# k and q of six attention units loaded in 2-KB packets and transposed by products with columns of the identity, two-bank score operations, early weight stores moved later, and a new opening order

## Chip, core and metric

The kernel runs on one core of one Trainium2 chip. The metric is the device time of one execution in microseconds (us).

## What is computed

```
a   = softmax over each 64-token chunk of q k^T / 8        q, k, v: 4 x 8 heads x 576 x 64, fp32
x   = a v, heads put side by side                          2304 tokens x 512
y   = ((x w_a) * (x w_b)) w_out                            512 -> 1536 -> 512
out = (P(h) / (Q(h) + 1e-6)) w_out2,  h = y w_in2          512 -> 2048 -> 512
```

P is a cubic polynomial of h, Q a quadratic one of |h|.

## The kernel before

All matmuls of the two MLPs are done in three products of a high and a low part (mm3, L251 to L253). TensorE (PE) is the engine that this keeps busy for nearly the whole program.

Tokens are handled in 18 units of 128 (two chunks of 64, all 8 heads). For a unit, `a_load` (L324) fetches k, q and v as [128 tokens, 8 heads, 64], so each packet is one head's 64 numbers of one token: 256 bytes. `a_transpose` (L333, L335) turns k and q into [head pair and d, token] with four 128x128 transposes on PE and one ACT copy out of PSUM. `a_scores` (L350) makes the scores with 16 products of 64x64 into two PSUM banks, a and b; DVE takes the maximum and subtracts it, once per bank (L356, L358). Then come the exponential (ACT, L364), sum, reciprocal and scaling (DVE, L369 to L372), the transposition of the probabilities (L380, L382) and the product with v (`a_pv`, L397), whose result is split into x_hi (ACT, L402) and x_lo (DVE, L406).

Units 0 to 2 make the first 384 tokens. The first product of the first MLP (L251, tile ab) needs all three of them and the first weight tile. Units 3 to 5 are done between products of ab, the later units in pairs (a_scores2, L430 to L438; a_pv2, L473).

A weight tile (512 KB) is loaded by SP (L170), recombined from its fp32 words and split in four pieces (`w_piece`: ACT L216, L218, L225; DVE L220, L223, L233; then L192 and L197 as hi and lo). Its recombined copy w_x is stored to DRAM by POOL (L235) right away, 256 KB each, since a later stage reads it back (L600).

The order of the opening is written out by hand in two strings. LOADS is the order of SP's first transfers (w is the next weight tile). FIRST is the order in which the pieces are issued: kN, qN are transpositions, SN scores, XN exponential, EN the rest of the softmax, PN transposition, VN product with v, LN the low part, w a weight piece, dN N dummy products (L898) on PE, +kN a load. Behind FIRST, work is queued with a due time (`later`, `todo`), and `tick` runs what is due; `half` lets 0.5 of that time pass after each half of an ab product. Each engine runs its own instructions in the order of issue.

Of the kernel before, what the change touches and what calls it, by code (L numbers as in the profile page):

```python
# [9 lines left out]
F32 = mybir.dt.float32  # L10
F32R = mybir.dt.float32r
I32 = mybir.dt.int32
# [3 lines left out]
ALU = mybir.AluOpType  # L16
# [4 lines left out]
def chunk_attention_two_mlps(  # L21
# [57 lines left out]

    FIRST = "k0 q0 w w d2 S0 w X0 w k1 E0 d2 q1 S1 w X1 P0 k2 w q2 E1 V0 w S2 X2 L0 w d2 P1 w V1 d4 +k5 E2 +v4 +q5 +v3 w w L1 P2 d2 +v5 w V2 d4 w L2 w w".split()  # L80
    LOADS = "k0 q0 w k1 q1 w v0 k2 q2 v1 w w v2 k3 q3 k4 q4".split()

    AHEAD = 4
    NWP = 12 - AHEAD
# [17 lines left out]
    ps_acc = ctx.enter_context(tc.tile_pool(name="ps_acc", bufs=4, space=PSUM))  # L102
    ps_ab = ctx.enter_context(tc.tile_pool(name="ps_ab", bufs=1, space=PSUM))
    ps_at = ctx.enter_context(tc.tile_pool(name="ps_at", bufs=2, space=PSUM))

    y_d = dram.tile([P, KD, NT], F32, name="y_d", tag="y_d")
# [87 lines left out]
    def w_lo(n):  # L194
        if n in f32s:
            hi, lo = wt[order[n]]
            nc.vector.tensor_tensor(lo, f32s.pop(n).bitcast(F32), hi.bitcast(F32), ALU.subtract)  # L197
            whole.add(order[n])

    def w_piece():  # L200

# [60 lines left out]
    def later(dt, f):  # L262
        todo.append((now[0] + dt, n_todo[0], f))
        n_todo[0] += 1
# [35 lines left out]
    def a_load(u, *names):  # L300

        (b0, c0), (b1, c1) = divmod(2 * u, NCH), divmod(2 * u + 1, NCH)
        for nm, src in (("k", k), ("q", q), ("v", v)):
# [19 lines left out]
            for dst, s in parts:  # L323
                nc.sync.dma_start(out=dst, in_=s.rearrange("h s d -> s h d"))  # L324
            raw[nm, u] = t

    def a_transpose(u, nm):

        t = raw.pop((nm, u)).rearrange("p (a b) d -> p a (b d)", b=2)
# [55 lines left out]
    def a_pv(u):  # L385

        pT, vv = un.pop(("pT", u)), raw.pop(("v", u))
        ps = []
        for c in range(2):
            pool, tag = (ps_acc, "acc") if u < UH else (ps_ab, "ab"[c])  # L390
            ps.append(pool.tile([P, HP, CH], F32, name="at", tag=tag))
        for hp in range(HP):
            a, t = divmod(hp, 2)
            for c in range(2):
                for h2 in range(2):
# [3 lines left out]
                    )  # L399
        out = [[t[:, :, u * P + c * CH:u * P + (c + 1) * CH] for t in (x_hi, x_lo)] for c in range(2)]  # L400
        for c, (hi, lo) in enumerate(out):
            nc.scalar.copy(hi, ps[c])  # L402
# [16 lines left out]
    def a_scores2(u):  # L419

        qT, kT = un["both", "qT"], un["both", "kT"]
        ps = [ps_ab.tile([P, 2, HP, CH], F32, name="at", tag=tag) for tag in "ab"]
        for x in range(2):
# [10 lines left out]
        e = a_both(u, "e").rearrange("p u x (y d) -> p u (x y) d", d=CH).rearrange("p u (b x) d -> p u b x d", b=2)  # L434
        for b in range(2):
            nc.vector.tensor_reduce(m[:, b], ps[b], AX.X, ALU.max)
        for b in range(2):
            nc.vector.tensor_tensor(  # L438
                e[:, :, b], ps[b], m[:, b].unsqueeze(3).to_broadcast([P, 2, HP, CH]), ALU.subtract
            )  # L440
# [72 lines left out]
    def x_second(g):  # L513
# [450 lines left out]
    def s_begin():  # L964

        nonlocal p_j2
        s_t.close()
        p_j2 = s_t.enter_context(tc.tile_pool(name="j2", bufs=1, side="right", reuse_waits="tile"))
        s_load(0)
        s_load(1)  # L970
# [175 lines left out]
```

## Time and profile before

| | us |
|---|---|
| median of 3 runs | 891.0 |
| lowest, highest | 889.84, 893.25 |
| the profiled execution, its own time | 891.69 |
| its span in the trace | 889.9 |
| PE busy | 872.8 (98%) |
| DVE, ACT busy | 717.8 (81%), 609.9 (69%) |

The profiled execution is the one that the trace shows; its own time is the span and 1.8 us around it, and it lies 0.7 us over the median. Shares of busy time are means over stages with different limits: the opening (to about 25 us) is a chain through all engines, and behind it PE hardly ever waits.

### The profile page before, as it was taken

What the parts mean: (1) busy time and instruction counts of PE and PEld (TensorE: products, weight loads), DVE (VectorE), ACT (ScalarE), POOL (GpSimd) and SP (SyncE); (2) the same over time, 40 slices, a digit from 0 to 9 for tenths busy, and PEclk for the clock granted to TensorE, in tenths of its full rate; (3) what the DMA queues carried; (4) which work ended last, traced back from release to release, by engine and by line L of the source; (5) the groups of instructions that cost most, each with busy time, mean ns of one, the idle gap of its engine ahead of it and who ended that gap; (6) DMA issues with size and microseconds to landing.
All of it is one profiled execution on the core that took longest, in us unless ns stands there. A gap on an engine that the chain in (4) does not pass through costs nothing.

```text
span 889.9 us, 14704 instructions
## 1 busy us (share of the span) xinstructions
PE 872.8 (98%) x5528; PEld 782.3 (88%) x5528; DVE 717.8 (81%) x1273; ACT 609.9 (69%) x1091; POOL 64.6 (7%) x122
## 2 busy tenths in 40 slices
PE   5989999999999999999999999999999999999998
PEld 4889999999999999888888998888888888888997
DVE  6757896767887885578877699999889888988886
ACT  6867987444555443577886788877677767776875
POOL 0112121111111111000100000000000000000000
PEclk9999999999999999999999999999999999999999
DMA  9999985134443335478876200200020002000100
GB/s 242 256 292 267 263 236 159 69 119 148 131 148 124 125 105 192 133 255 280 287 267 233 72 1 1 83 1 1 1 95 1 1 1 84 0 1 1 48 1 36
DMA packets 107335, 105.82 MB, mean 119 GB/s; under 512 B 61440, under 2 KB 84480, under 8 KB 107264
## 3 DMA queue, kind: packets, MB, share of 16 engines
q1 hardware_dynamic: 99264, 79.71, 30.3%
q0 software_dynamic: 8000, 25.17, 7.5%
q8 instruction: 43, 0.70, 0.3%
q14 instruction: 28, 0.23, 0.1%
HBM read 74.98 MB, written 29.88 MB: 118 GB/s over the span
## 4 chain that ended last, share of the span: by engine, by line
PE 93%; ACT 2%; DMA 2%; DVE 1%; SPq 1%; issue 0%; ACTq 0%
PE h L251 7%; PE h L253 7%; PE h L252 7%; PE acc L253 7%; PE acc L252 7%; PE acc L251 7%; PE acc L765 5%; PE acc L766 5%; PE acc L768 5%; PE ab L251 3%; PE ab L252 3%; PE ab L253 3%; PE y L252 3%; PE y L253 3%; PE y L251 3%; PE q L251 2%
## 5 line engine op out<-in xcount | busy, mean ns | idle before, releaser
L253 PE MATMUL h<-y,w_i 128*128 128x512 f32 (+1 forms) x320 | 117.7, 368 | 0.0
L251 PE MATMUL h<-y,w_i 128*128 128x512 f32 (+1 forms) x320 | 117.7, 368 | 0.0
L252 PE MATMUL h<-y,w_i 128*128 128x512 f32 (+1 forms) x320 | 117.6, 368 | 0.0
L823 ACT ACTIVATE a_ring<-h 128x512 f32<-128x512 f32 (+1 forms) x80 | 44.1, 551 | 85.9 <-PE h L253 85.9
L662 ACT COPY s<-y 128x384 f32<-128x384 f32 x72 | 34.5, 480 | 85.2 <-PE y L253 85.0
L765 PE MATMUL acc<-g_hi,w_o 128*128 128x512 f32 (+1 forms) x240 | 86.4, 367 | 0.0
L766 PE MATMUL acc<-g_hi,w_o 128*128 128x512 f32 (+1 forms) x240 | 86.2, 367 | 0.0
L826 DVE SCALAR_TENSOR_TENSOR u<-u,cb_t,a_ring 128x512 f32<-128x512 f32 (+1 forms) x80 | 55.6, 695 | 29.4 <-ACT u L824 28.8
L252 PE MATMUL acc<-w_o,g_hi 128*128 128x512 f32 x191 | 74.4, 390 | 0.0
L253 PE MATMUL acc<-w_o,g_lo 128*128 128x512 f32 x191 | 74.4, 389 | 0.0
L251 PE MATMUL acc<-w_o,g_hi 128*128 128x512 f32 x191 | 74.3, 389 | 0.0
L251 PEld LDWEIGHTS h<-y,w_i 128*128 128x128 f32 x320 | 60.1, 188 | 8.6
L252 PEld LDWEIGHTS h<-y,w_i 128*128 128x128 f32 x320 | 60.0, 188 | 8.6
L253 PEld LDWEIGHTS h<-y,w_i 128*128 128x128 f32 x320 | 60.1, 188 | 7.6
L745 DVE TENSOR_TENSOR g_lo<-g_raw,g_hi 128x512 fp32r<-128x512 f32 (+1 forms) x60 | 38.2, 638 | 30.8 <-PE acc L768 15.0
L768 PE MATMUL acc<-g_lo,w_o 128*128 128x512 f32 (+1 forms) x240 | 59.0, 367 | 0.0
L825 ACT ACTIVATE t<-h,ca_t 128x512 f32<-128x512 f32 (+1 forms) x80 | 59.0, 737 | 0.0
L836 DVE SCALAR_TENSOR_TENSOR u<-u,r 128x512 f32<-128x512 f32 (+1 forms) x80 | 50.6, 632 | 9.1 <-ACT r L835 9.1
L828 DVE SCALAR_TENSOR_TENSOR t<-t,ca_t,h 128x512 f32<-128x512 f32 (+1 forms) x80 | 55.6, 695 | 2.8
L835 ACT ACTIVATE r<-r,nlsh 128x512 f32<-128x512 f32 (+1 forms) x80 | 54.5, 682 | 2.6
L834 ACT ACTIVATE r<-u,nlsh 128x512 f32<-128x512 f32 (+1 forms) x80 | 55.5, 694 | 0.5
L837 DVE SCALAR_TENSOR_TENSOR t<-t,ca_t,r 128x512 f32<-128x512 f32 (+1 forms) x80 | 55.4, 692 | 0.0
(210 smaller groups left out, 2380.6 us busy)
## 6 DMA issues: line engine op xcount, KB each, us to landing
w_raw<-in_moe_w_out_dram SPq DMA_DIRECT2D x28, 512.0 KB, 3.9
g_d<-g POOLq DMA_DIRECT2D x72, 192.0 KB, 2.5
g_raw<-g_d SPq DMA_DIRECT2D x48, 256.0 KB, 4.0
w_raw<-in_moe_w_in_dram SPq DMA_DIRECT2D x16, 512.0 KB, 4.2
w_raw<-in_moe_w_a_dram SPq DMA_DIRECT2D x12, 512.0 KB, 5.7
w_raw<-in_moe_w_b_dram SPq DMA_DIRECT2D x12, 512.0 KB, 5.5
out_dram<-o SPq DMA_DIRECT2D x18, 256.0 KB, 2.3
y_d<-ys POOLq DMA_DIRECT2D x16, 256.0 KB, 3.5
```

The source lines that it names most:

```text
L251: nc.tensor.matmul(ps, wh, xh, start=first, stop=False, **kw)
L252: nc.tensor.matmul(ps, wh, xl, start=False, stop=False, **kw)
L253: nc.tensor.matmul(ps, wl, xh, start=False, stop=last, **kw)
L765: nc.tensor.matmul(acc[j][d], wh, gh, start=i == 0, stop=False)
L766: nc.tensor.matmul(acc[j][d], wl, gh, start=False, stop=False)
L768: nc.tensor.matmul(acc[j][d], cols(w, d)[0], gl, start=False, stop=i == F1 - 1)
L825: nc.scalar.activation(t, ps, AF.Identity, scale=ca_t[:, 3:4], bias=ca_t[:, 2:3])
L826: nc.vector.scalar_tensor_tensor(u, u, cb_t[:, 0:1], ah, ALU.add, ALU.mult)
L828: nc.vector.scalar_tensor_tensor(t, t, ca_t[:, 1:2], ps, ALU.add, ALU.mult)
L834: nc.scalar.activation(r, u, AF.Ln, scale=2.0 ** -LSH, bias=nlsh[:, 0:1])
L835: nc.scalar.activation(r, r, AF.Exp, scale=-1.0, bias=nlsh[:, 1:2])
L837: nc.vector.scalar_tensor_tensor(t, t, ca_t[:, 0:1], r, ALU.add, ALU.mult)
```

## The change

1. **2-KB rows.** With KQ = 6, units 0 to 5 load k and q with partition = (head, group of 8 tokens) and 8 tokens x 64 numbers in a row, 2 KB in one piece. The source's access pattern is then 8 heads x 16 groups x 512 numbers (8 x 8 x 512 for the halves of unit 4, which lies over two batches), where it was 128 tokens x 8 heads x 64. v and the other units load as before.
2. **Transposition by products.** Such a tile is turned by 16 plain products (8 tokens of a group x 2 halves) of the tile's 128 x 64 column block with 64 columns of the identity, in place of four transposes. Each writes 64 partitions of the bank; the two halves of a pair write the lower and the upper 64. The ACT copy reads PSUM with a step of 64 numbers to put the tokens back in order.
3. **Two-bank operations.** Scores go to one tile of two banks. One DVE maximum and one subtraction of 512 numbers replace two of 256 each; in pairs one maximum of 1024 replaces two of 512. x_hi and x_lo of units 3 to 5 become one operation each.
4. **Stores later.** The w_x of the first 8 weight tiles are held in rooms of the X pool (w_room), and their stores are queued for time 9 + n.
5. **Order.** New FIRST and LOADS; the operations of `x_second` for the groups of units before the last are paced over 14 half-steps, not 13.

```diff
-    FIRST = "k0 q0 w w d2 S0 w X0 w k1 E0 d2 q1 S1 w X1 P0 k2 w q2 E1 V0 w S2 X2 L0 w d2 P1 w V1 d4 +k5 E2 +v4 +q5 +v3 w w L1 P2 d2 +v5 w V2 d4 w L2 w w".split()
-    LOADS = "k0 q0 w k1 q1 w v0 k2 q2 v1 w w v2 k3 q3 k4 q4".split()
+    FIRST = "k0 q0 w d2 w w S0 w X0 k1 E0 d2 q1 S1 w X1 P0 w k2 q2 E1 V0 w S2 L0 d2 w X2 P1 d2 w +k5 E2 w +v4 +v3 V1 +q5 d4 w w L1 P2 d2 +v5 V2 d4 w L2 w w w".split()
+    LOADS = "k0 q0 w k1 q1 w v0 k2 v2 k3 q2 v1 w k4 q3 w q4".split()
+    KQ = 6
...
+    def w_room(n):
+
+        if n >= NWP:
+            return p_io.tile([P, DM], I32, name="w_x", tag="io")
+        if n % 3 == 0:
+            rooms[n // 3] = p_X.tile([P, 3, DM], I32, name="w_x", tag=f"X1_{(7, 6, 4)[n // 3]}")
+        return rooms[n // 3][:, n % 3]
...
-            x = f32s[n] = p_io.tile([P, DM], I32, name="w_x", tag="io")
+            x = f32s[n] = w_room(n)
             nc.vector.tensor_tensor(x, c, z, ALU.add)
             if key in w1_d:
-                nc.gpsimd.dma_start(out=w1_d[key], in_=x.bitcast(F32))
+                def store():
+                    nc.gpsimd.dma_start(out=w1_d[key], in_=x.bitcast(F32))
+
+                if n < NWP:
+                    todo.append((9 + n, n_todo[0], store))
+                    n_todo[0] += 1
+                else:
+                    store()
...
-                nc.sync.dma_start(out=dst, in_=s.rearrange("h s d -> s h d"))
+                if nm == "v" or u >= KQ:
+                    nc.sync.dma_start(out=dst, in_=s.rearrange("h s d -> s h d"))
+                elif b0 == b1:
+                    nc.sync.dma_start(
+                        out=dst.rearrange("p h d -> p (h d)"), in_=s.rearrange("h (g j) d -> h g (j d)", j=H)
...
-        for hp in range(HP):
-            nc.tensor.transpose(ps[:, hp, :], t[:, hp, :], ident)
         o = a_tmp(u, nm + "T") if u < 2 * UH else a_both(u, nm + "T")[:, u % 2]
-        nc.scalar.copy(o, ps)
+        if u >= KQ:
+            t = t.rearrange("p (a b) d -> p a (b d)", b=2)
+            for hp in range(HP):
+                nc.tensor.transpose(ps[:, hp, :], t[:, hp, :], ident)
+            nc.scalar.copy(o, ps)
+        else:
+
+            same = 2 * u // NCH == (2 * u + 1) // NCH
+            ps = ps.rearrange("p a (x y) -> p (a x) y", x=2)
+            if same:
+                eye = ident.rearrange("p (a b g) -> p b a g", a=HP, b=2)
+            else:
+                eye = ident.rearrange("p (c a b g) -> p b a c g", c=2, a=HP, b=2)
+            for j in range(H):
+                for b in range(2):
+                    r = slice(b * CH, (b + 1) * CH)
+                    nc.tensor.matmul(ps[r, j], t[:, j], eye[:, b], start=True, stop=True)
+            nc.scalar.copy(o.rearrange("p a (g j) -> p (a g) j", j=H), ps.rearrange("p j y -> p y j"))
...
+    def two_banks(n):
+
+        t = ps_two.tile([P, 2, 2 * HP, CH], F32, name="at", tag="two")
+        return t[:, :, :n * HP], [t[:, b, :n * HP] for b in range(2)]
...
-        ps = [ps_ab.tile([P, HP, CH], F32, name="at", tag=tag) for tag in "ab"]
+        two, ps = two_banks(1)
...
-        for b in range(2):
-            nc.vector.tensor_reduce(m[:, b], ps[b], AX.X, ALU.max)
-        for b in range(2):
-            nc.vector.tensor_tensor(
-                e[:, b], ps[b], m[:, b].unsqueeze(2).to_broadcast([P, HP, CH]), ALU.subtract
-            )
+        nc.vector.tensor_reduce(m, two, AX.X, ALU.max)
+        nc.vector.tensor_tensor(e, two, m.unsqueeze(3).to_broadcast([P, 2, HP, CH]), ALU.subtract)
...
-            pool, tag = (ps_acc, "acc") if u < UH else (ps_ab, "ab"[c])
-            ps.append(pool.tile([P, HP, CH], F32, name="at", tag=tag))
+        if u >= 3:
+            two, ps = two_banks(1)
+        else:
+            pool, tag = (ps_acc, "acc") if u < UH - 0 else (ps_at, "at")
+            ps = [pool.tile([P, HP, CH], F32, name="at", tag=tag) for c in range(2)]
...
-            later(at + 0.5 * (n * (9 if g == NQ - 1 else 13) // len(ops)) + (1.5 if g == NQ - 1 and n >= 7 else 0), f)
+            later(at + 0.5 * (n * (9 if g == NQ - 1 else 14) // len(ops)) + (1.5 if g == NQ - 1 and n >= 7 else 0), f)
```

SP's queue from its seventh transfer on, that is v of unit 0, before (kqv is the tile of a unit's k, q or v, w_raw that of a weight):

```order
L324 DMA kqv<-in_v_dram 128x8x64
L324 DMA kqv<-in_k_dram 128x8x64
L324 DMA kqv<-in_q_dram 128x8x64
L324 DMA kqv<-in_v_dram 128x8x64
L170 DMA w_raw<-in_moe_w_a_dram 128x4x256
L170 DMA w_raw<-in_moe_w_b_dram 128x4x256
```

and now:

```order
L345 DMA kqv<-in_v_dram 128x8x64
L347 DMA kqv<-in_k_dram 128x1x512
L345 DMA kqv<-in_v_dram 128x8x64
L347 DMA kqv<-in_k_dram 128x1x512
L347 DMA kqv<-in_q_dram 128x1x512
L345 DMA kqv<-in_v_dram 128x8x64
L173 DMA w_raw<-in_moe_w_a_dram 128x4x256
L351 DMA kqv<-in_k_dram 64x1x512 x2
```

q of unit 2, the third row before, is now the fifth: v of unit 2 and k of unit 3 go ahead of it. The weight tile that was the fifth row is now the seventh.

PE's first instructions before (at is a PSUM tile; t holds kT, qT or the probabilities of a unit, ident is the identity):

```order
L333 MATMUL at<-ident,kqv 128x128 x8
L898 MATMUL at<-ident 128x128 x2
L350 MATMUL at<-t_144 64x64 x16
L333 MATMUL at<-ident,kqv 128x128 x4
L898 MATMUL at<-ident 128x128 x2
L333 MATMUL at<-ident,kqv 128x128 x4
L350 MATMUL at<-t_145 64x64 x16
```

and now:

```order
L378 MATMUL at<-ident,kqv 64x64 x32
L947 MATMUL at<-ident 128x128 x2
L399 MATMUL at<-t_144 64x64 x16
L378 MATMUL at<-ident,kqv 64x64 x16
L947 MATMUL at<-ident 128x128 x2
L378 MATMUL at<-ident,kqv 64x64 x16
L399 MATMUL at<-t_145 64x64 x16
```

Nothing changes its place here; each transposition of four instructions became one of sixteen (the size shown is that of the result). Between the products of ab the transpositions of units 3 to 5 stand where they stood.

POOL's first stores before (w_a and w_b in DRAM are written from w_x):

```order
L235 DMA w_a_118<-w_x 128x512
L235 DMA w_b_119<-w_x 128x512
L235 DMA w_a_120<-w_x 128x512
L576 DMA g_d_83<-g 128x384
L235 DMA w_b_121<-w_x 128x512
L235 DMA w_a_122<-w_x 128x512
L576 DMA g_d_84<-g 128x384
```

and now:

```order
L625 DMA g_d_83<-g 128x384
L625 DMA g_d_84<-g 128x384
L625 DMA g_d_85<-g 128x384
L625 DMA g_d_86<-g 128x384
L249 DMA w_a_118<-w_x 128x512
L249 DMA w_a_126<-w_x 128x512
L625 DMA g_d_83<-g 128x384
L249 DMA w_b_119<-w_x 128x512
L249 DMA w_a_120<-w_x 128x512
L249 DMA w_b_127<-w_x 128x512
```

The first store of a weight tile now follows the fourth store of g, and the stores of the first eight tiles alternate with those of the later ones.

## Rows read from the trace of the kernel before

**Rows 1.** Windows by stage: us; busy of PE, PEld, DVE, ACT, POOL; clock; DMA share; GB/s

```profile
0.00:25.00 25.00, 15.55 (x261) 12.79 (x261) 15.89 (x41) 15.78 (x30) 2.38 (x9) 1.00 1.01 242
25.00:40.00 15.00, 14.96 (x177) 13.68 (x177) 10.86 (x27) 12.27 (x23) 1.70 (x4) 1.00 0.95 254
40.00:56.00 16.00, 13.07 (x162) 10.78 (x162) 10.46 (x23) 10.94 (x24) 2.70 (x5) 1.00 1.00 294
56.00:150.00 94.00, 93.27 (x1251) 88.84 (x1252) 75.71 (x125) 77.93 (x140) 16.93 (x31) 1.00 0.88 243
```

**Rows 2.** Waits of PE, 25 to 150 us: us in total, times, longest

```profile
PE at L333 <- DMA kq<-in_k_dram: 1.5, 1, 1.5
PE at L333 <- DMA q<-in_q_dram: 0.9, 1, 0.9
PE ab L251 <- ACT w_b L192: 0.4, 1, 0.4
```

**Rows 3.** Timeline of PE, opening: start, us, operation [idle before it, what ended it]

```profile
4.08 1.09 PE L333 MATMUL at<-ident,kqv 128*128 128x128 f32 x4 [4.08 <-DMA kqv<-in_k_dram]
5.60 1.12 PE L333 MATMUL at<-ident,kqv 128*128 128x128 f32 x4 [0.43 <-DMA kqv<-in_q_dram]
...
7.50 1.13 PE L350 MATMUL at<-t 64*64 64x64 f32 x32
...
13.81 1.27 PE L333 MATMUL at<-ident,kqv 128*128 128x128 f32 x8 [0.44 <-DMA kqv<-in_k_dram]
...
16.70 0.69 PE L350 MATMUL at<-t 64*64 64x64 f32 x32 [0.80 <-ACT t L335]
...
24.95 0.42 PE L251 MATMUL ab<-x_hi,w_a 128*128 128x384 f32 x1
```

**Rows 4.** Timeline of ACT, opening

```profile
6.75 0.58 ACT L335 COPY t<-at 128x512 f32<-128x512 f32 x1 [0.96 <-PE at L333]
7.55 0.79 ACT L216 ACTIVATE w_a<-w_raw 128x512 f16<-128x512 f32 x1 [0.21 <-DMA w_raw<-in_moe_w_a_dram]
```

**Rows 5.** Timeline of DVE, opening

```profile
12.61 0.76 DVE L356 TENSOR_REDUCE m<-at 128x4 f32<-128x256 f32 x2
13.28 0.75 DVE L358 TENSOR_TENSOR t<-at,m 128x256 f32<-128x256 f32 x2
...
20.05 0.68 DVE L369 TENSOR_REDUCE s<-t 128x8 f32<-128x512 f32 x1
...
21.23 0.69 DVE L372 TENSOR_TENSOR t<-t,s 128x512 f32<-128x512 f32 x1
```

**Rows 6.** Timeline of PE between the first products of ab

```profile
26.34 1.03 PE L333 MATMUL at<-ident,kqv 128*128 128x128 f32 x8
27.13 0.42 PE L251 MATMUL ab<-x_hi,w_a 128*128 128x384 f32 x1
...
28.26 0.60 PE L333 MATMUL at<-ident,kqv 128*128 128x128 f32 x4
28.79 0.69 PE L350 MATMUL at<-kT,qT 64*64 64x64 f32 x32
29.41 0.44 PE L251 MATMUL ab<-x_hi,w_b 128*128 128x384 f32 x1
```

**Rows 7.** Instructions of L350, 0 to 60 us: ns min/median/max, first and last start

```profile
L350 PE MATMUL at<-kT,qT x96: 218/218/267, 28.8 to 38.2; 64*64 64x64 f32 x96
```

**Rows 8.** DMA view, 10.5 to 12.5 us (packets of 256 bytes)

```profile
DMA packets 1780, 0.45 MB, mean 225 GB/s; under 512 B 1776, under 2 KB 1780, under 8 KB 1780
```

**Rows 9.** DMA view, 656.5 to 661 us (packets of 2 KB): packets, share

```profile
DMA packets 799, 1.46 MB, mean 324 GB/s; under 512 B 88, under 2 KB 88, under 8 KB 799
...
q1 hardware_dynamic: 799, 1.46, 97.4%
```

**Rows 10.** DMA view, 0 to 60 us: issues, KB, median us to landing

```profile
w_a<-w_x POOLq DMA_DIRECT2D x4, 256.0 KB, 5.6
```

More of the change, by code (lines that the diff above doesn't have):

```diff
@@ L102, in chunk_attention_two_mlps @@
     ps_acc = ctx.enter_context(tc.tile_pool(name="ps_acc", bufs=4, space=PSUM))
-    ps_ab = ctx.enter_context(tc.tile_pool(name="ps_ab", bufs=1, space=PSUM))
     ps_at = ctx.enter_context(tc.tile_pool(name="ps_at", bufs=2, space=PSUM))
+    s_two = ctx.enter_context(ExitStack())
+    ps_two = s_two.enter_context(tc.tile_pool(name="ps_two", bufs=1, space=PSUM))
+    ps_ab = None
     y_d = dram.tile([P, KD, NT], F32, name="y_d", tag="y_d")
@@ L198, in w_lo @@
             whole.add(order[n])
+    rooms = {}
+    def w_room(n):
[4 more added lines that the diff above has]
+        return rooms[n // 3][:, n % 3]
     def w_piece():
@@ L323, in a_load @@
             for dst, s in parts:
-                nc.sync.dma_start(out=dst, in_=s.rearrange("h s d -> s h d"))
+                if nm == "v" or u >= KQ:
[3 more added lines that the diff above has]
+                        out=dst.rearrange("p h d -> p (h d)"), in_=s.rearrange("h (g j) d -> h g (j d)", j=H)
+                    )
+                else:
+                    nc.sync.dma_start(
+                        out=dst.rearrange("p h d -> p (h d)"), in_=s.rearrange("h (g j) d -> h g (j d)", j=H)
+                    )
@@ L325, in a_load @@
             raw[nm, u] = t
     def a_transpose(u, nm):
-        t = raw.pop((nm, u)).rearrange("p (a b) d -> p a (b d)", b=2)
+        t = raw.pop((nm, u))
         pool, tag = (ps_acc, "acc") if u < UH else (ps_at, "at")
         ps = pool.tile([P, HP, P], F32, name="at", tag=tag)
-        for hp in range(HP):
-            nc.tensor.transpose(ps[:, hp, :], t[:, hp, :], ident)
         o = a_tmp(u, nm + "T") if u < 2 * UH else a_both(u, nm + "T")[:, u % 2]
-        nc.scalar.copy(o, ps)
+        if u >= KQ:
[15 more added lines that the diff above has]
+            nc.scalar.copy(o.rearrange("p a (g j) -> p (a g) j", j=H), ps.rearrange("p j y -> p y j"))
@@ L387, in a_pv @@
         pT, vv = un.pop(("pT", u)), raw.pop(("v", u))
-        ps = []
-        for c in range(2):
-            pool, tag = (ps_acc, "acc") if u < UH else (ps_ab, "ab"[c])
-            ps.append(pool.tile([P, HP, CH], F32, name="at", tag=tag))
+        if u >= 3:
+            two, ps = two_banks(1)
+        else:
+            pool, tag = (ps_acc, "acc") if u < UH - 0 else (ps_at, "at")
+            ps = [pool.tile([P, HP, CH], F32, name="at", tag=tag) for c in range(2)]
         for hp in range(HP):
@@ L400, in a_pv @@
         out = [[t[:, :, u * P + c * CH:u * P + (c + 1) * CH] for t in (x_hi, x_lo)] for c in range(2)]
+        if u >= 3:
+            out = [[t[:, :, u * P:(u + 1) * P].rearrange("p k (c d) -> p c k d", c=2) for t in (x_hi, x_lo)]]
+            ps = [two]
         for c, (hi, lo) in enumerate(out):
@@ L421, in a_scores2 @@
         qT, kT = un["both", "qT"], un["both", "kT"]
-        ps = [ps_ab.tile([P, 2, HP, CH], F32, name="at", tag=tag) for tag in "ab"]
+        two, ps = two_banks(2)
+        ps = [t.rearrange("p (x h) d -> p x h d", x=2) for t in ps]
         for x in range(2):
@@ L434, in a_scores2 @@
         e = a_both(u, "e").rearrange("p u x (y d) -> p u (x y) d", d=CH).rearrange("p u (b x) d -> p u b x d", b=2)
-        for b in range(2):
-            nc.vector.tensor_reduce(m[:, b], ps[b], AX.X, ALU.max)
-        for b in range(2):
+        nc.vector.tensor_reduce(m, two.rearrange("p b (u x) d -> p b u x d", u=2), AX.X, ALU.max)
+        for x in range(2):
             nc.vector.tensor_tensor(
-                e[:, :, b], ps[b], m[:, b].unsqueeze(3).to_broadcast([P, 2, HP, CH]), ALU.subtract
+                e[:, x], two[:, :, x * HP:(x + 1) * HP], m[:, :, x].unsqueeze(3).to_broadcast([P, 2, HP, CH]), ALU.subtract
             )
@@ L964, in s_begin @@
     def s_begin():
-        nonlocal p_j2
+        nonlocal p_j2, ps_ab
         s_t.close()
+        s_two.close()
+        ps_ab = ctx.enter_context(tc.tile_pool(name="ps_ab", bufs=1, space=PSUM))
         p_j2 = s_t.enter_context(tc.tile_pool(name="j2", bufs=1, side="right", reuse_waits="tile"))
```

## Prediction, made before the changed kernel was run

> **What bounds the kernel now.** I read the stages first. From 56 us on PE is busy all but 0.7 of 94 us, with the granted clock at 1.00 (2.4 GHz) [rows 1], so nothing there is to be had by faster transfers. Two stretches are different. Up to 25 us PE, DVE and ACT are each busy for under 16 us: a chain. From 25 to 56 us PE lacks 0.04 us and then 2.93 us, with the DMA share at 0.95 to 1.00 [rows 1]. The waits of PE tell whose: 1.5 us for a k, 0.9 us for a q, 0.4 us for the hi part of a weight that ACT makes [rows 2], together 2.8 us. So the whole change can win those 2.8 to 2.9 us and what it gets out of the opening; against it stands whatever it adds to PE, which from 25 us on adds to the time one for one.
>
> The opening on PE [rows 3]: k of unit 0 lands and is turned at 4.08 us, q at 5.60 us after a 0.43 us wait, the scores start at 7.50 us, k and q of unit 2 are turned at 13.81 us, its scores start at 16.70 us, the first product of ab at 24.95 us. The transposition before the first scores takes 1.09 us, one at 28 us 0.60 us [rows 3, 6]: the first rows run at about half the speed of the later ones (1.8 times), although the clock's column says 1.00.
>
> **The transposition, between the products of ab.** k and q of units 3 to 5, six transpositions, stand between products of ab, where PE has no gap but the three waits. Before, each costs 0.40 us: two of them from 26.34 us to the next product at 27.13 us is 0.79 us [rows 6]. New, each is 16 products with 64 moving columns and all 128 rows. No row shows such a product. The nearest is the scores' product, 64x64, also plain fp32: 16 of them, 32 records, take 0.69 us, of which the last 0.22 us is the run-out of one (0.218 us each), so they start over 0.47 us [rows 6, 7]. These use a quarter of the array each. Were four at a time the rule, four take 0.47 / 4 = 0.117 us, and a product holds its quarter for 0.117 us. The new product holds a half (both row halves of one column half), so two run side by side, and 16 take 8 x 0.117 = 0.94 us. Bounds: 0.47 us if they start as fast as the 64x64 ones, 16 x 0.117 = 1.88 us if they run one after another. I take 0.94 us, since it is the same row with the share of the array counted. Going into another shape of product and out of it also costs: from the transposition at 28.26 us to the scores at 28.79 us is 0.53 us and from those to ab at 29.41 us 0.62 us [rows 6], 0.13 and 0.15 us more than the starts of 0.40 and 0.47 us. That happens in four or five places (two places turn two tiles at once, one stands directly before scores and saves one step), some 0.15 us each: 0.7 us. Sum: 6 x 0.94 + 0.7 - 6 x 0.40 = **+3.9 us**, bounds +1.1 and +9.6 us.
>
> The rows show that scores in the same row half but in the other column half do overlap, or 32 records could not start in 0.47 us [rows 6]. The Trainium skill, "TensorE: Matmul & The Clock Gate", section "Packing small matmuls: row/col tiling", says that a weight load overlaps products in flight only if it goes to another row group. The new products all use every row group, so by that rule the halves would run one after another. It is the second rival below.
>
> **The opening.** With 0.36 us less for each tile (below) k of unit 0 can be turned from 3.7 us on and q lands by 4.9. Each transposition takes 0.94 x 1.8 = 1.7 us there: 3.7, 5.4, 7.1 us. ACT's copy took 0.58 us at 6.75 us [rows 4]; with the strided read it takes that or, as the strided 16-bit operation with 0.79 us behind it [rows 4], a little more. The scores then start at 7.9 to 8.2 us, in place of 7.50: **+0.5 us** (bounds -0.8, if the products start four at a time, and +3.5, if one at a time). From there DVE paces: nothing arrives for it before 7.55 us [rows 4], and of the 17.4 us behind that it is busy for 15.9 [rows 1]. Four more transpositions lie on PE, which idles for 5 of the 21 us behind its first row [rows 1, 3], so they cost nothing unless a set of scores is late; their strided copies lie on ACT, idle for as long. The two-bank operations: two maxima and two subtractions of 256 numbers run from 12.61 to 14.03 us, 1.42 us [rows 5]; a sum of 512 numbers takes 0.68 us and a scaling 0.69 us [rows 5], so one after the other 1.37 us, as the subtraction has to wait for the whole maximum. Three units: 0.15 us at most, costed at **0**. New FIRST: weight pieces change places with the same pieces; **0**, with 0.5 us either way, since DVE's order decides what waits.
>
> **Transfers.** 256 KB in 256-byte packets go at 225 GB/s, 1.17 us [rows 8], in 2-KB packets at 324 GB/s, 0.81 us [rows 9]: 0.36 us less for each of 12 tiles, 4.3 us. The eight stores of 256 KB that leave the first 56 us [rows 10] free 0.8 us each, 6 us. The three waits lie behind this queue, the latest by 1.5 us, and PE itself asks up to 4 us later. All three go: **-2.9 us**. What is late next? q of unit 2 now has v of unit 2 and k of unit 3 ahead of it, 1.17 + 0.81 us; six faster tiles ahead of it and itself save 6 x 0.36 = 2.2 us. So it lands where it did, in time for 13.8 us [rows 3]. The stores' due times, 9 to 16, put them at some 63 to 93 us (an estimate from where the halves of ab stand in the timeline), where the DMA share is 0.88 on average [rows 1]; 2 MB at 324 GB/s is 6.5 us more. The cover is that loads run ahead there: PE's waits in those 94 us are 0.7 us in all. Cost **0**; if a load were late for each, 1 to 3 us. POOL only issues, and g's stores no longer stand behind a w_x. Held rooms, the merged x_lo, the pairs' maximum and the pacing over 14 half-steps change DVE's and ACT's order where PE has work: 0.
>
> **Sum**, against the profiled execution (891.7 us): 3.9 + 0.5 - 2.9 = +1.5, 893.2 us. That execution lies 0.7 us over the median, so **892.5 us** for the median.
>
> **Rivals.** (1) *The new loads use half of the DMA engines.* A 2-KB packet takes 16 engines x 0.974 x 4.5 us / 799 = 88 ns [rows 9]; 128 of them on 8 engines are 1.41 us for a tile, slower than before. Then q of unit 2 lands 6 x 0.24 + 1.17 + 1.41 = 4.0 us later, less a store, 3.4 us; its scores start some 2.7 us behind 16.70 us, and so does ab. Sum 2.7 + 3.9 - 2.9 = +3.7: 894.7 us for the median. For it: the outermost dimension of the source is now 8 where it was 128. Against: no row shows a load of that form. The Trainium skill, "DMA: Bandwidth & Descriptors", section "Why a DMA increments its semaphore by 16 and not by 1", lets a transfer use the largest number of engines up to 16 that divides the slowest dimension on both sides, which would be 8 here.
>
> (2) *Slower: the column halves run one after another.* Place: every transposition of units 0 to 5 on PE. Price 1.88 us in place of 0.94: +9.6 us between the ab products, and 2 x 1.7 us more before the first scores, 3.5 to 4; less 2.9: +10.6, 901.6 us for the median. It decides from 1.4 us a tile on, where the sum passes +4.5 us. Against it the overlap seen in rows 6, for it that those products share rows with a neighbour of other row groups.
>
> (3) *The products start as fast as 64x64 ones.* +1.1 in place of +3.9 and -0.8 in the opening, -2.9: -2.6, 888.4 us for the median. Only this wins, and by less than 0.5%.
>
> **How the numbers follow.** The forecast's case 0.50, half of the engines 0.27, one after another 0.10, cheap products 0.13. A measurement of this kernel can tell about 0.5% (4.5 us) from no change, so faster means under 886.5, slower over 895.5 us. Faster: a part of the last case with a further gain, 0.06. Slower: all of the second rival, half of the first and a little of the rest: 0.22. Same: 0.72. The range, 888.2 to 898 us, leaves out the second rival and the lower part of the third.
>
> **What would show it.** Right: rows of the new transposition at 0.9 to 1.1 us per tile between ab products, PE without waits for DMA from 25 to 56 us, the first scores near 8.0 and ab near 25.4 us, the span 1 to 2 us longer. Half of the engines: k and q land later than v of the same size, and q of unit 2 holds PE at 14 to 18 us. Wrong in the main: a tile at 0.5 or at 1.9 us; PE waiting for loads between 60 and 95 us beside the stores; DVE's x_lo or maximum before ab's start later than PE needs.

## The result: 900.5 us, 1.0% slower

The changed kernel takes 900.5 us (median of 4 runs, 898.86 to 900.87) beside 892.1 us for the kernel before in the same job; the ratio is 1.010, its 95% interval 1.0083 to 1.0116. That is outside the range given. The profiled execution took 898.86 us, its span is 897.1 us in place of 889.9. The medians below leave out one execution of e1_g_outer (1103 us, the one that was profiled) and one of e4_warm (1263 us), which ran at mean granted clocks of 0.75 and 0.66.

The windows of the changed kernel, columns as in [rows 1] (us; busy time of PE, PEld, DVE, ACT and POOL; granted clock; DMA share; GB/s):

```profile
0.00:25.00 25.00, 15.56 (x337) 14.17 (x338) 9.71 (x21) 10.68 (x18) 0.69 (x6) 0.89 0.82 207
25.00:40.00 15.00, 14.46 (x249) 12.84 (x247) 9.59 (x20) 10.19 (x20) 0.00 (x0) 0.96 0.84 219
40.00:56.00 16.00, 15.20 (x251) 13.56 (x250) 13.30 (x27) 14.67 (x27) 1.22 (x2) 1.00 0.99 256
56.00:150.00 94.00, 93.87 (x1273) 89.67 (x1273) 73.43 (x116) 76.49 (x138) 20.17 (x37) 1.00 0.89 253
```

Behind 56 us nothing is lost: PE lacks 0.13 us of 94. In the first 25 us DVE does 9.7 us of work in place of 15.9, and the granted clock is 0.89 in place of 1.00. The timeline of PE in the opening, to be held against [rows 3]:

```profile
4.98 3.81 PE L378 MATMUL at<-ident,kqv 128*64 128x64 f32 x64 [4.98 <-DMA kqv<-in_k_dram]
...
9.53 0.69 PE L399 MATMUL at<-t 64*64 64x64 f32 x32
...
15.67 1.15 PE L378 MATMUL at<-ident,kqv 128*64 128x64 f32 x32 [0.44 <-DMA kqv<-in_k_dram]
20.05 1.97 PE L378 MATMUL at<-ident,kqv 128*64 128x64 f32 x32 [3.23 <-DMA kqv<-in_q_dram]
...
22.86 1.08 PE L399 MATMUL at<-t 64*64 64x64 f32 x32
...
31.52 0.42 PE L271 MATMUL ab<-x_hi,w_a 128*128 128x384 f32 x1
```

k of unit 0 is turned at 4.98 us (before 4.08), the first scores start at 9.53 (7.50), q of unit 2 comes 3.23 us after PE could have turned it, its scores start at 22.86 (16.70), and the first product of ab at 31.52 (24.95). So 6.57 of the 7.2 us by which the span grew are lost before ab. From there to the end it is 865.6 us, before 865.0: +0.6.

What PE meets between the products of ab:

```profile
32.99 2.09 PE L378 MATMUL at<-ident,kqv 128*64 128x64 f32 x64
35.01 0.44 PE L271 MATMUL ab<-x_hi,w_a 128*128 128x384 f32 x1
...
36.25 1.15 PE L378 MATMUL at<-ident,kqv 128*64 128x64 f32 x32
37.34 0.69 PE L399 MATMUL at<-kT,qT 64*64 64x64 f32 x32
```

From the start of two transpositions to the next product it is 2.02 us, from the start of one 1.09 us: 1.0 us a tile where [rows 6] had 0.40. The waits of PE from 25 to 150 us, which answer to [rows 2]:

```profile
PE ab L273 <- DVE w_b L200: 0.8, 1, 0.8
PE at L443 <- ACT pT L427: 0.4, 1, 0.4
```

The three waits for DMA are gone; a wait of 0.8 us for the lo part of a weight, which DVE makes, is new.

Why q of unit 2 is late is told by SP's queue and by the landing records. The timeline of SP (start, duration of the issue):

```profile
5.10 3.69 SPq L347 DMA_DIRECT2D kqv<-in_k_dram  x1
8.84 1.40 SPq L345 DMA_DIRECT2D kqv<-in_v_dram  x1
10.28 3.09 SPq L347 DMA_DIRECT2D kqv<-in_k_dram  x1
13.42 0.61 SPq L347 DMA_DIRECT2D kqv<-in_q_dram  x1
```

The issue of k of unit 2 is held up for 3.7 us, that of k of unit 3 for 3.1 us, and q of unit 2, behind them, is issued at 13.42 us. Issues were held up before the change too (that of q of unit 2 stood from 8.90 to 10.97 us), so this alone is no sign of slow loads. The records of a load's semaphore, one for each piece that has landed, tell on how many engines it ran. k of unit 0, times in us:

```
before   3.60 3.62 3.64 3.64 3.65 3.65 3.67 3.67 3.75 3.76 3.79 3.79 3.81 3.85 3.87 3.95
changed  1.91 4.27 4.27 4.41 4.49 4.60 4.61 4.79 4.84
```

Sixteen before; now one 0.4 us behind the issue, too early for data (the first record of k of unit 0 came at 3.25 us or later in the kernels that had sixteen), and eight more: half of the DMA engines. A weight tile, which still has sixteen records, lands in two halves now: eight records at 9.49 to 10.41 us and eight at 12.79 to 13.27, as it would behind eight loaded and eight free engines. The last record of each of the first loads, us, here and in kernels of the next section (k0 is k of unit 0, w a weight tile; between v0 and q2 the order of the loads differs, and k2 and q2 alone are shown; PE cannot turn a tile before its last record):

```
                    k0    q0    w     k1    q1    w     v0    k2    q2
before              3.95  5.56  7.53  8.67  9.72 11.29 12.49 13.67 14.38
changed             4.84  6.77  8.27 10.30 11.99 13.27 14.01 15.53 20.00
e2_kq0              4.06  5.47  7.58  8.59  9.45 11.02 12.22 13.43 17.04
e3_q2_first         5.33  7.44  8.96 11.04 12.51 13.67 14.84 16.34 17.88
e7_kq0_q2           3.93  5.01  7.51  8.59  9.45 11.25 12.44 13.64 14.84
e5_16eng            4.40  5.38  7.51  8.69  9.75 11.21 12.86 13.86 18.37
```

The granted clock is the third piece. Windows of the changed kernel around the wait:

```profile
15.00:18.00 3.00, 1.39 (x35) 1.04 (x32) 2.50 (x7) 1.96 (x5) 0.00 (x0) 1.00 0.91 243
18.00:20.00 2.00, 0.00 (x0) 0.00 (x0) 1.28 (x2) 0.27 (x1) 0.00 (x0) 0.83 1.03 211
20.00:22.00 2.00, 1.95 (x36) 1.84 (x36) 0.00 (x0) 0.00 (x0) 0.00 (x0) 0.50 0.98 303
24.00:26.00 2.00, 2.00 (x10) 2.00 (x11) 1.96 (x4) 0.98 (x3) 0.00 (x0) 0.50 0.88 190
```

PE stands still from 16.8 to 20.05 us, and then works at a granted clock of 0.50 (1.2 GHz) until 26: the transposition of q of unit 2 takes 1.97 us where that of k took 1.15.

### The profile page after: what moved, and what is told of

It reads as the page before. It is cut to its first block, busy times and chain, and to the rows that moved or that the text cites. A ratio compares the mean times of both kernels' runs of the same rounds, so it can differ in the third digit from the quotient of the medians.

```text
span 897.1 us, 15347 instructions
## 1 busy us (share of the span) xinstructions
PE 881.8 (98%) x5868; PEld 792.3 (88%) x5868; DVE 717.5 (80%) x1252; ACT 610.7 (68%) x1088; POOL 64.4 (7%) x122
## 4 chain that ended last, share of the span: by engine, by line
PE 96%; SPq 1%; DVE 1%; DMA 1%; ACT 1%; issue 0%; ACTq 0%
PE h L271 7%; PE h L272 7%; PE h L273 7%; PE acc L272 7%; PE acc L271 7%; PE acc L273 7%; PE acc L814 5%; PE acc L815 5%; PE acc L817 5%; PE ab L271 4%; PE ab L273 4%; PE ab L272 4%; PE y L271 3%; PE y L272 3%; PE y L273 3%; PE q L271 2%
## 5 line engine op out<-in xcount | busy, mean ns | idle before, releaser
L625 POOL DMA_DIRECT2D g_d<-g x72 | 39.4, 548 | 244.7 <-DVE g L629 93.6
```

## Experiments

Theory A: half of the DMA engines for the 2-KB loads make q of unit 2 late. Theory B: its place behind two more tiles does. Theory C: the longer transpositions make the opening long. "ab" is the start of ab's first product and "behind" the time from there to the end of the span, both of the one profiled execution. "Old" and "new" are FIRST and LOADS of before and of the change; "q2 early" has q of unit 2 loaded directly behind k of unit 2. The kernels ran in several jobs, in which the kernel before had medians of 891.0 to 892.1 us; a ratio is always to the kernel before in the same job, with its 95% interval.

| kernel | k, q by | order | median us | ab | behind |
|---|---|---|---|---|---|
| before | 256 B | old | 891.0 to 892.1 | 24.95 | 865.0 |
| changed | 2 KB, 8 engines | new | 900.5 | 31.52 | 865.6 |
| e2_kq0 | 256 B | new | 891.3 | 27.70 | 861.7 |
| e3_q2_first | 2 KB, 8 | new, q2 early | 896.3 | 28.21 | 865.4 |
| e7_kq0_q2 | 256 B | new, q2 early | 890.4 | 26.40 | 861.8 |
| e9_kq0_old_order | 256 B | old | 889.5 | 24.54 | 863.7 |
| e10_old_order | 2 KB, 8 | old | 897.8 | 30.27 | 866.9 |
| e11_late_only | 256 B | old | 890.0 | 24.66 | 864.1 |
| e12_q2_first_kq3 | 2 KB, 8, units 0 to 2 | new, q2 early | 892.9 | 28.94 | 861.9 |
| e5_16eng | 2 KB, 16 | new | 899.1 | 29.76 | 866.6 |
| e6_16eng_q2 | 2 KB, 16 | new, q2 early | 897.9 | 31.43 | 865.7 |
| e8_16eng_q2_kq3 | 2 KB, 16, units 0 to 2 | new, q2 early | 891.5 | 27.88 | 861.9 |
| e13_fewer_dummies | 2 KB, 16 | new, q2 early | 895.8 | 27.54 | 865.3 |
| e4_warm | 2 KB, 8 | new | 900.3 | 32.27 | 867.6 |
| e14_warm13 | 2 KB, 8 | new | 899.7 | 31.55 | 865.7 |
| e15_unit0_old | 2 KB, 8, not unit 0 | new | 899.2 | 31.27 | 865.8 |

**Loads and order apart.** e2_kq0 is the changed kernel with `KQ = 0`.

> The changed kernel without its 2-KB loads and products (k and q of all units as 128 x 8 x 64 and four transposes); order, late stores and two-bank operations stay. Theory A: opening as in the kernel before within 1 us (first product of ab at 24.5 to 26.5 us), transpositions of 0.4 us between the products of ab, DMA waits of PE from 25 to 56 us smaller than 2.9 us because the stores are gone; time 2 to 4 us under the kernel before. Theory B: q of unit 2 is late by 1 to 2 us here too, time 1 us under to 2 us over the kernel before. Theory C: as A.

891.29 us, ratio 0.9996 (0.9987 to 1.0006). Theories A and B were each half right: with sixteen engines PE still waits 2.90 us for q of unit 2, the clock falls (0.86 in the first 25 us), and ab starts 2.75 us later than before; the rest of the 6.57 us needs the 2-KB loads or their products. And the stage behind is 3.3 us shorter than before. PE's timeline in e2_kq0:

```profile
17.09 1.11 PE L365 MATMUL at<-ident,kqv 128*128 128x128 f32 x4 [2.90 <-DMA kqv<-in_q_dram]
...
19.04 1.08 PE L399 MATMUL at<-t 64*64 64x64 f32 x32
```

e3_q2_first:

```diff
-    LOADS = "k0 q0 w k1 q1 w v0 k2 v2 k3 q2 v1 w k4 q3 w q4".split()
+    LOADS = "k0 q0 w k1 q1 w v0 k2 q2 v2 k3 v1 w k4 q3 w q4".split()
```

> The changed kernel with q of unit 2 loaded directly behind k of unit 2, ahead of v of unit 2 and k of unit 3; loads on eight engines as in the change. Theory A: k of unit 0 still turned at 5 us and the first scores at 9.5 us; q of unit 2 lands near 17.3 us in place of 20.0, its scores start near 19.5, ab near 28.5; time 2.5 to 4 us under the changed kernel, still 4 to 6 us over the kernel before. Theory B: the opening is as before within 1 us (ab at 26), time 5.5 us or more under the changed kernel.

896.32 us, 4.2 under the changed kernel, ratio 1.006 (1.0044 to 1.0077). As A expected for ab (28.21); q lands at 17.88 us and the clock stays at 1.00. e7_kq0_q2 is e3_q2_first with `KQ = 0`.

> The changed kernel with 256-byte loads and transposes for all units (as e2_kq0), and q of unit 2 loaded directly behind k of unit 2: what is left of the change is the late stores, the two-bank operations and the rest of the order. Order theory: q of unit 2 lands near 14.6 us, no 2.9-us wait and no fall of the clock, ab at 24.7 to 25.5 us, the stage behind 3.2 us shorter than in the kernel before as in e2_kq0; time 888 to 889, 2.5 to 3.5 us under the kernel before. If the stage behind only gained because the later start gave the loads time: DMA waits of PE come back between 25 and 56 us, time 890.5 to 891.5.

890.44 us, ratio 0.9991 (0.998 to 1.0001): less than expected, since ab starts at 26.40. Beside e2_kq0, which differs in the place of q of unit 2 alone, that is 1.30 us earlier: so much does the place cost at ab's start, and what else is new in the order costs more (1.86 us, by the next kernel). The stage behind keeps its 3.2 us. Between e7_kq0_q2 and e3_q2_first only loads and products differ: 5.9 us. e9_kq0_old_order has `KQ = 0` and FIRST and LOADS of before.

> The changed kernel with 256-byte loads and transposes for all units and with FIRST and LOADS of the kernel before: the late stores, the two-bank operations and the pacing are left. If these shorten the stage behind ab's start by the 3.2 us that e2_kq0 and e7_kq0_q2 show (863.2 - 861.7 and so on against 864.9 us from ab's first product to the end) and the old opening keeps ab at 24.5 to 25.3 us: time 887.5 to 889, 2 to 3.5 us under the kernel before. If the gain behind was only the reverse of a later start (loads had more time): DMA waits of PE of over 1.5 us between 25 and 56 us, time 890 to 891.5.

889.46 us, ratio 0.9972 (0.9963 to 0.9982): 2.0 us faster than the kernel before, the lowest median of all. ab starts at 24.54 us, 3.16 us earlier than with the new order (e2_kq0). Of the gain behind ab 1.2 us are left, not 3.2: with the earlier start the loads have less time, and a wait for q of unit 4 appears, whose last record comes at 27.59 us:

```profile
PE at L365 <- DMA kqv<-in_q_dram: 1.2, 1, 1.2
PE ab L273 <- DVE w_b L200: 0.8, 1, 0.8
PE at L399 <- DVE e L405: 0.4, 1, 0.4
```

So both of its cases hold in part. e10_old_order has FIRST and LOADS of before and the loads of the change.

> The changed kernel with FIRST and LOADS of the kernel before; k and q of six units on eight engines and turned by products, as in the change. First scores at 9.3 to 10.6 us (k of unit 0 lands late, two transpositions of 1.9 us each), q of unit 2 lands near 17 us, ab at 27 to 28.5 us; time 895 to 897, that is 4 to 5.5 us under the changed kernel: the order's part. If the order has no part beside the loads: 899 to 901.

897.84 us, ratio 1.0071 (1.0056 to 1.0087). The old order wins 2.7 us back, the loads and products cost 8.4 us beside e9_kq0_old_order. The two causes do not add up: at ab's start the new order costs 3.16 us with 256-byte loads and 1.25 us with 2-KB loads (30.27 to 31.52), the loads and products 5.73 us in the old order and 3.82 us in the new. In the profiled execution, the slowest of the four, k and q of unit 2 land at 17.79 and 20.11 us, 1.5 and 2.2 later than in e3_q2_first behind the same loads; why is open.

**The late stores alone.** e11_late_only is the kernel before with `w_room` and the queued store, and nothing else of the change.

> The kernel before with the late stores alone (rooms for w_x, stores queued for time 9 + n). If the late stores are what shortens the stage behind ab's start: PE's three waits for DMA between 25 and 56 us (2.9 us) shrink to under 1 us, ab's start within 0.5 us of 24.95, no new waits from 60 to 95 us beside 0.8 us; time 888 to 889.2. If the 2-KB loads or the two-bank operations were needed for that: 890 to 891.5.

890.01 us, ratio 0.9979 (0.997 to 0.9988): the late stores by themselves win 1.5 us of the 2.0 of e9_kq0_old_order. The gain is under what was expected: a wait of 0.8 us for w_b's lo part comes with them, and 0.6 us of waiting for a q stay. No wait for DMA appears between 60 and 95 us, here or in the changed kernel: the stores are covered there.

**The products between those of ab.** e12_q2_first_kq3 is e3_q2_first with `KQ = 3`.

> As e3_q2_first, with the 2-KB loads and products for units 0 to 2 alone. The same opening as e3_q2_first (ab at 28 to 28.5 us), and between the products of ab transposes of 0.40 us in place of products of 1.0 us a tile: time 3.4 to 4.4 us under e3_q2_first, 892 to 893. If the products between those of ab cost less than the rows say, or if the 256-byte loads of units 3 to 5 bring waits for DMA back: less than 2.5 us under it.

892.89 us, 3.4 under e3_q2_first; behind ab 861.9 in place of 865.4. No wait for DMA came back. The six transpositions of units 3 to 5, with their loads, cost 3.4 to 3.5 us.

**Sixteen engines.** e1_g_outer:

```diff
-                        out=dst.rearrange("p h d -> p (h d)"), in_=s.rearrange("h (g j) d -> h g (j d)", j=H)
+                        out=dst.rearrange("p h d -> p (h d)"), in_=s.rearrange("h (g j) d -> g h (j d)", j=H)
-                eye = ident.rearrange("p (a b g) -> p b a g", a=HP, b=2)
+                eye = ident.rearrange("p (g a b) -> p b a g", a=HP, b=2)
```

> The changed kernel with one thing different: the unsplit k and q tiles are loaded with the 16 token groups as the outermost dimension (partition = group, head in place of head, group), same 2-KB packets, same number of products. Theory A (the loads with outermost dimension 8 run on half of the DMA engines, so each takes longer and q of unit 2 is late): landing records come in sixteen again, k of unit 0 is turned by 4.2 us, q of unit 2 before 16.5 us, no 3.2-us wait and no fall of the granted clock at 19 us; the first product of ab at 25 to 26.5 us in place of 31.5; time 5 to 6.5 us under the changed kernel, 893.5 to 896. Theory B (the place of q of unit 2 behind v of unit 2 and k of unit 3 is to blame): q of unit 2 still waits for over 2 us, time within 1.5 us of the changed kernel. Theory C (the slower transpositions make the opening long): q lands in time, ab still starts after 29 us.

901.01 us; against A. But its products now read identity columns 8 numbers apart, and such a transposition took 2.08 us beside 0.77 for scores (its only trace, at a granted clock of 0.75). Only the records are used: k of unit 0 has sixteen. e5_16eng reads the columns in one piece:

```diff
+    ident_g = const.tile([P, P], F32, name="ident_g")
+    nc.vector.tensor_copy(ident_g.rearrange("p (x g) -> p x g", x=H), ident.rearrange("p (g x) -> p x g", x=H))
-                eye = ident.rearrange("p (g a b) -> p b a g", a=HP, b=2)
+                eye = ident_g.rearrange("p (a b g) -> p b a g", a=HP, b=2)
```

> The changed kernel with the k and q tiles that lie in one batch loaded group by group (outermost dimension 16, landing records sixteen, as in e1_g_outer) and with an identity whose columns are put in head order by one early DVE copy, so that the products read 16 columns in one piece, as in the change. The order of loads stays. Half-engine theory alone: q of unit 2 in time, no wait, ab at 25.5 to 26.5 us, time 893.5 to 896. Order theory alone: as the changed kernel, 900. Both (each costs about half): k of unit 0 turned at 4.4 to 4.6 in place of 5.0 to 5.4 us, q of unit 2 lands near 17.9 us in place of 20.0, ab at 28.5 to 29.5 us, time 896.5 to 898.5.

899.1 us, 1.4 under the changed kernel by medians but only 0.3 beside the kernel before of each job (ratio 1.0094, 1.0069 to 1.0119): not clear of noise. The loads are as fast as 256-byte ones again, no faster (the table of records), and q of unit 2 still comes late. But something new stands in the way. PE's timeline in e5_16eng:

```profile
14.53 0.74 PE L380 MATMUL at<-ident_g,kqv 128*64 128x64 f32 x17
16.94 0.68 PE L380 MATMUL at<-ident_g,kqv 128*64 128x64 f32 x15 [1.67 <-issue]
18.42 1.40 PE L380 MATMUL at<-ident_g,kqv 128*64 128x64 f32 x32 [0.79 <-DMA kqv<-in_q_dram]
```

In the middle of one tile, all of it landed at 13.86 us, PE stops for 1.67 us, with nothing that the profile shows to wait for. e6_16eng_q2 is e5_16eng with LOADS of e3_q2_first, e8_16eng_q2_kq3 that with `KQ = 3`.

> The same as e5_16eng, and q of unit 2 loaded directly behind k of unit 2. Both causes undone: q of unit 2 lands near 15.8 us, no wait of over 0.5 us for it and no fall of the clock, ab at 25.8 to 26.8 us, what is left over the kernel before is the slower transposition in front of the first scores (1 to 1.5 us) and the sum of the stage behind (+1); time 893 to 894.5. If the transpositions by products were the larger part of the loss (theory C): ab after 28 us, 896 or more.

897.94 us (894.44 to 898.9, the last of them profiled): 4 us more than expected. The tile is there at 13.76 us and q of unit 2 at 14.84, PE stops behind the same record for 2.58 us, and the clock falls to 0.50 twice, at 20 to 22 and at 26 to 28 us:

```profile
14.36 0.74 PE L380 MATMUL at<-ident_g,kqv 128*64 128x64 f32 x17
17.68 1.90 PE L380 MATMUL at<-ident_g,kqv 128*64 128x64 f32 x47 [2.58 <-issue]
```

> The same as e6_16eng_q2 with the 2-KB loads and products for units 0 to 2 alone; units 3 to 5 by 256-byte rows and transposes. ab at 25.8 to 26.8 us as in e6_16eng_q2, and no products with columns of the identity between the products of ab: the stage behind 3 to 4 us shorter than in e6_16eng_q2; time 889.5 to 890.5. If 2-KB loads of units 3 to 5 were what took the DMA waits away: waits of over 1 us come back and the time is 891 or more.

891.50 us, ratio 1.0 (0.999 to 1.0011); the same stop behind record 17, for 0.42 us. With both causes taken out, the 2-KB loads and the products of units 0 to 2 still cost 1.1 us beside e7_kq0_q2 of the same job (intervals overlap), and ab starts 1.48 us later: that is what is left for theory C in this kernel. Its neighbour on eight engines is e12_q2_first_kq3, ratio 1.0021 (1.001 to 1.0032): half of the engines cost 1.4 to 1.9 us there.

The stops come next. Three kernels stop at one instruction, whatever has landed, and in each the only 16-KB packet of the instruction queue of this stretch is under way shortly before. The DMA view of e5_16eng, 13 to 17 us:

```profile
q1 hardware_dynamic: 1685, 0.88, 118.8%
q8 instruction: 1, 0.02, 2.3%
```

It is read as PE's program being loaded behind full DMA queues: the packet starts at 13.98 us there and at 10.60 in the changed kernel, where eight engines had room. e13_fewer_dummies takes the dummies out of e6_16eng_q2 that stand ahead of this place:

```diff
-    FIRST = "k0 q0 w d2 w w S0 w X0 k1 E0 d2 q1 S1 w X1
+    FIRST = "k0 q0 w w w S0 w X0 k1 E0 q1 S1 w X1
```

> As e6_16eng_q2 without the two pairs of dummy products ahead of the transposition of k of unit 2: 4 products, in records 8 weight loads and 8 products fewer on PE before that place. If PE stands still there because the next piece of its program is not loaded, it stops at the same instruction count: 8 product records later, behind record 25 in place of 17 of that transposition. If it waits for the tile or for a PSUM buffer, it stops at the first record, or where it did.

895.81 us, 2.1 us less, ab at 27.54 against 31.43 (the slowest execution of e6_16eng_q2 beside the fastest here). PE doesn't stop at all: it comes to the place at 16.4 us, 1.5 us later than e6_16eng_q2 (14.9), with the packet through at 14.6. Part of that is a second effect: without the dummies the products of unit 1 run at 1.84 us a tile in place of 1.15. So the run fits the reading, but the stop at record 25 that would have settled it was not seen.

The traces settle it. PE's records (products, weight loads and those of its sequencer) can be counted up to each stop of over 0.35 us that the profile puts down to "issue". In all 17 traces there are eight:

```
                 records ahead  stop  ends at  16-KB packet ended
e5_16eng                   449  1.67    16.94               15.43
e6_16eng_q2                449  2.58    17.68               16.37
e8_16eng_q2_kq3            449  0.42    16.34               14.77
e5_16eng                   705  0.60    25.33               23.96
e6_16eng_q2                705  0.93    25.42               23.90
e1_g_outer                 705  0.88    26.26               24.76
e4_warm                    962  0.52    33.63               32.04
e10_old_order             2497  0.81    83.95               82.48
```

The counts lie 256 or a multiple of it apart, to within one record, although the kernels have different instructions there:

```profile
25.33 0.69 PE L445 MATMUL at<-pT,kqv 64*64 64x64 f32 x29 [0.60 <-issue]
33.63 0.44 PE L273 MATMUL ab<-x_hi,w_a 128*128 128x384 f32 x1 [0.52 <-issue]
```

The first is of e5_16eng, the second of e4_warm (below). Each stop ends 1.3 to 1.6 us after a 16-KB packet, and at the first six such places no kernel, with a stop or without, goes on sooner than 1.3 us after the packet of that place. So a packet brings PE the next 256 records of its program, and PE stops where it is late. In the kernel before, with 4 transposes in place of 16 products, PE came to record 449 only at 22.64 us, 3.6 us behind the packet.

**The clock.** e4_warm and e14_warm13 put dummies into the wait:

```diff
-    FIRST = "... P0 w k2 q2 E1 ..."
+    FIRST = "... P0 w k2 d20 q2 E1 ..."
```

(d13 in the second.)

> The changed kernel with 20 dummy products between the transpositions of k and q of unit 2, so that PE is busy while it waits for q. If the fall of the granted clock to 0.5 at 19 to 26 us comes from PE's idle stretch and costs time, the clock stays at 1.0, the transposition of q of unit 2 takes 1.15 us in place of 1.97 and ab starts 0.8 to 1.3 us earlier (30.3 to 30.7 us), the time falls by about as much. If the clock has no part, the time is the changed kernel's within 0.4 us.

> As e4_warm with 13 dummy products (about 3 us) in place of 20, so that they end where q of unit 2 lands. If the fall of the clock costs time: no clock of 0.5 behind 9 us, the transposition of q of unit 2 takes 1.15 us, from its start to ab's first product 10.1 us as in e4_warm in place of 11.5 in the changed kernel, ab 1 to 1.4 us earlier, time 899 to 899.6. If not: the changed kernel's time within 0.5 us.

900.26 and 899.67 us. In both the clock stays at 1.00, and from the transposition of q of unit 2 to ab it is 10.13 and 10.11 us, in the changed kernel 11.47: the fall costs 1.35 us. The time shows little of it. The 20 dummies gave all of it back by running to 22.2 us, 1.4 us past the landing (20.72); with 13 the time is 0.8 us lower, not clear of noise, and ab's start in the profiled execution is not earlier, as q of unit 2 landed at 21.02 in place of 20.00. PE's timeline in e14_warm13:

```profile
18.34 3.17 PE L947 MATMUL at<-ident 128*128 128x128 f32 x26
21.44 1.15 PE L378 MATMUL at<-ident,kqv 128*64 128x64 f32 x32
```

**The first scores.** e15_unit0_old:

```diff
-                if nm == "v" or u >= KQ:
+                if nm == "v" or u >= KQ or u == 0:
-        if u >= KQ:
+        if u >= KQ or u == 0:
```

> The changed kernel with k and q of unit 0 by 256-byte rows and transposes (sixteen engines), all else as in the change. First scores back at 7.0 to 7.6 us in place of 9.5. If q of unit 2 sets ab's start: it still lands late (18.5 to 19.5 us, less than 1.5 us earlier), PE waits 4 us or more for it, ab at 30 to 31 us, time 898.5 to 900. If the first scores set it: ab at 29 to 29.6 us, time 898 or less.

899.19 us, ab at 31.27. The first scores are 2.4 us earlier and ab 0.25 us:

```profile
7.14 1.13 PE L399 MATMUL at<-t 64*64 64x64 f32 x32
...
19.80 1.97 PE L378 MATMUL at<-ident,kqv 128*64 128x64 f32 x32 [3.55 <-DMA kqv<-in_q_dram]
```

So q of unit 2 sets ab's start, and not the first scores: their lateness is covered by the wait for it.

## Why the prediction was wrong

**The stage behind ab was right.** The transpositions: 16 products in 1.0 us, forecast 0.94; behind ab they cost +3.5 us (e12_q2_first_kq3 beside e3_q2_first) to +3.9 us (the changed kernel beside e2_kq0), forecast +3.9. The two column halves run side by side: in the changed kernel's transposition at 36.25 us their records start in pairs, 7 ns apart, a pair every 58 ns. One after another they would have taken 1.88 us by the prediction's estimate, so the second rival is out. What the Trainium skill, "TensorE: Matmul & The Clock Gate", section "Packing small matmuls: row/col tiling", states of weight loads, that they overlap products in flight only if they go to another row group, is not borne out here: all these products use every row group. The waits for DMA went, as forecast; that a wait of 0.8 us for DVE would come was not foreseen. Sum behind ab: forecast +1.0, measured +0.6. In part that was luck: the late opening gave the loads time. With 256-byte loads and ab at 24.5 to 24.7 us, 1.2 us (e9_kq0_old_order) and 0.6 us (e11_late_only) of waiting for DMA stayed; no run has 2-KB loads and so early an ab.

**The stores were right in cover, too high in price.** Nothing waited for them at 60 to 95 us. By themselves they are worth 1.5 us, half of the 2.9 that they and the faster loads were to win.

**The opening failed: +0.5 forecast, +6.57 measured.** The step that failed is "So it lands where it did, in time for 13.8 us", with the "0.36 us less for each of 12 tiles" under it. Three things were wrong in it. First, the loads ran on eight engines. The first rival said that. I gave it 0.27 because no row of before showed such a load. The Trainium skill, "DMA: Bandwidth & Descriptors", section "Why a DMA increments its semaphore by 16 and not by 1", holds here: nine records with 8 outermost, sixteen with 16. Second, even on sixteen engines 2-KB rows gained nothing in this stretch: the seventh load lands at 12.86 us in e5_16eng and at 12.22 in e2_kq0. The 324 GB/s of [rows 9] came from a stretch with only one kind of load; the opening runs at 207 to 242 GB/s with either. From 2 to 12 us of e5_16eng a 2-KB packet took 134 ns on average, where the prediction had 88; what makes it longer there is open. Third, the place behind two tiles was to be paid for with that saving; alone it costs 2.2 us of landing (17.04 in e2_kq0, 14.84 in e7_kq0_q2).

**The first rival's price was too low**, 894.7 us. It had 1.41 us a tile, 16 packets of 88 ns on each of eight engines; between the landings of neighbouring tiles lie 1.7 and 1.9 us (10.30 to 11.99, 4.84 to 6.77), as a 2-KB packet took 112 ns on average there (2 to 12 us). It left out that tiles on all sixteen engines come later too, behind the loaded eight, and that the clock is halved after PE has stood still: 1.35 us. So q came 5.6 us late in place of 3.4, and with the clock that is 7.0 us; of these 0.4 were made up before ab, where is not shown. (Two sums of the prediction are a little off: 4.0 us less a store of 0.8 is 3.2, not 3.4, and all of the second rival with half of the first is 0.235 for slower, not 0.22. Neither changes the forecast.)

**The first scores** came 2.0 us late, forecast 0.5 (1.87 us a transposition, forecast 1.7; k 0.9 us later instead of 0.4 earlier). It cost 0.25 us, as q's lateness covers it.

**Two-bank operations** were costed at 0; e9_kq0_old_order less e11_late_only gives -0.55 us with the pacing, about what runs differ by.

From the fastest version to the changed kernel by medians: e9_kq0_old_order 889.5; new order +1.8 (e2_kq0, 891.3); products between those of ab +3.4; what remains, +5.8, is the 2-KB loads and products in the opening. It sums to 900.5 because the last term is what is left. How the 5.8 us divide is not shown: in the change's order sixteen engines won 1.4 us at most (e5_16eng), since q of unit 2 stayed late and PE's stops came in their place; with sixteen engines, q early and units 3 to 5 as before, 1.1 us are left (e8_16eng_q2_kq3 beside e7_kq0_q2). The version to keep is e9_kq0_old_order, the late stores and the two-bank operations without the rest; the late stores alone (e11_late_only) lie 0.55 us above it, within noise.

## What to carry to other kernels

Larger packets only pay if the load keeps all DMA engines and if the packets were the limit in that stretch: look at the outermost dimension of the access pattern, count the landing records, and take the rate from the same stretch, not from a quiet one. When a load is moved behind others, cost the wait of the one engine that needs it first, and add what the clock does after that engine has stood still. A term that a later wait covers costs next to nothing, and removing it wins next to nothing (0.25 us in e15_unit0_old). More instructions for an engine are more of its program to load, beside the data: where a profile shows a wait that ends for no visible reason, look for a packet of the instruction queue just before.

## What the runs showed of the hardware

A load on half of the engines slows the others: a weight tile's records came in two groups of eight, whose last ones are 2.9 us apart. PE stopped in mid-tile for 0.4 to 2.6 us where a 16-KB packet of the instruction queue was late; each packet brings 256 of PE's records (stops ahead of records 449, 705, 962 and 2497), and PE went on 1.3 us or more after the packet's end. A transposition whose moving columns lie 8 numbers apart was slower: in e1_g_outer 2.08 us at 36.75 us, where two of unit 4, with 8 numbers in a piece, took 2.50 us at 32.85, both at a granted clock of 0.75. Plain products with all 128 rows that alternate between the two column halves ran side by side: 16 in 1.0 us, in pairs of records 7 ns apart.
